# Banded attention in blocks of 32 by 32: a fused attention and MoE kernel on one Trainium2 core

## The chip, the cores and the metric

The kernel runs on one core of a Trainium2 chip. The core has a matrix engine (TensorE, "PE" in the profile, with its weight loads as "PEld"), a vector engine (VectorE, "DVE"), a scalar engine (ScalarE, "ACT"), a general engine (GpSimd, "POOL") and a sync engine (SyncE, "SP") that issues most of the transfers. Matrix products land in eight PSUM banks of 128 partitions by 512 f32 numbers; the other operands lie in SBUF, also 128 partitions. The metric is the device time of one execution in microseconds (us).

## The reference

There are 8 batches of 8 heads, 576 positions and 64 numbers per head. Each head computes two attentions, their sum goes into a feed-forward layer.

```python
# pooled: q, k, v averaged over groups of 4 positions (144 left), full softmax
out_up = np.repeat(sm_attn(q_d, k_d, v_d), 4, axis=2)
# banded: each query sees the keys less than 4 positions away
mask = np.abs(pos[:, None] - pos[None, :]) < 4
scores = np.where(mask, scale * np.matmul(q, k.transpose(0, 1, 3, 2)), -1000000000.0)
scores = scores - np.max(scores, axis=-1, keepdims=True)
attn = np.exp(scores)
attn = attn / (np.sum(attn, axis=-1, keepdims=True) + 1e-09)
x = out_up + np.matmul(attn, v)
# x as 4608 tokens of 512 numbers
h = x @ w_in                                  # 512 -> 2048
return (h * np.clip(h + 3.0, 0.0, 6.0) / 6.0) @ w_out
```

## The kernel before, in words

**Feed-forward layer.** The 4608 tokens go in nine chunks of 512 (`PART`). For each of 16 slices `f` of the 2048 hidden numbers, GEMM1 (`gemm1`, L981) makes a bank `h` from four pieces of the inner dimension, three matmuls each, because every f32 operand is split into a rounded high part and a low part. ACT and DVE apply the gate (L987, L991) and split the result again (L995, L999). GEMM2 (`gemm2`, L1031) adds four token tiles into banks `o0` to `o3`, three matmuls each. That is twelve matmuls of 128x512 per slice for either GEMM, 1728 in all for each. GEMM1 alternates between banks `h0` and `h1`.

**Attention.** A *unit* is one batch and one pair of heads, 32 units in all. The two heads of a unit lie side by side: head 0 in partitions 0 to 63, head 1 in 64 to 127. Batches reach the GEMMs in order: chunk 1 needs batch 1, and so on. `plan_unit` writes out one unit's operations. It knows two ways, set by `ALONE = 2`.

Batches 0 and 1 go *alone*: each step is its own operation. Pooled scores (`scores_d`, L455), banded scores (`scores`: L658 puts the mask into the bank as a matmul, L666 the products), turning the weights by PE (`trans_d` L548, `trans` L691), the two products with v (`pv_d` L633 or L636, `pv` L709), and for some value sums `sum_pe` (L418).

Batches 2 to 7 go by *bursts* (`plan_burst`): one operation on PE holds the scores of a new unit and the products with v of the unit two before it (`DEPTH = 2`), so that GEMMs are interrupted once for both. In it, `scores_d4` (L472) makes pooled scores, `pv` (L709) and `pv_d4` (L617) the products, `scores` (L666) the banded scores. Between a unit's first and second burst the weights are turned: the unnormalised scores become weights on DVE, ACT and POOL, are written to DRAM (`put_d`, `put`) and read back in pieces (`get_d`, `get`), and DVE turns 32x32 blocks (`turn_d` L584, `turn_l` L603). A burst takes `h0` and `h1` for products and a third of the pooled scores, and two more banks `a0` and `a1` for scores. At the change of batch group the pipeline runs full: the first two bursts have no old unit, and the last two no new one.

**The banded windows before.** Ten windows of 64 queries by 64 keys, 57 apart (`window`), cover 576 positions with a margin of three. Five lie in one half of the partitions and five in the other; with two heads that is 20 matmuls of 64 by 64 for the scores and 20 for the products. The softmax of batches 2 to 7 adds the mask while moving out of PSUM (`outside`, L682), takes the maximum over 64 keys (L511), and does one exponential per window with the maximum as bias and the sum as a by-product (`exps_sums`, L522: ten exponentials, ten accumulator reads). `norm` (L539) divides.

**The order of work.** Nothing is ordered by hand. `Plan` holds operations with engines to choose from, costs, resources (banks, SBUF slots) and due times; `emit` plays a schedule forward and writes the instructions in the order it finds. So a change to one cost or resource can reorder everything. `need` and `UNIT_T` set when a batch is due. The planner also models PE's instruction supply (`FETCH`, L1151, `fetch`), in records of matmuls (`rec`).

## Time and profile before

| | |
|---|---|
| median of 3 runs | 926.57 us (925.02 to 932.66) |
| profiled execution | 927.57 us |
| its span | 925.0 us |
| PE busy | 907.6 us (98%), 7045 matmul records |
| DVE busy | 552.5 us (60%) |
| ACT busy | 440.2 us (48%) |
| POOL busy | 233.8 us (25%) |
| DMA moved | 93.48 MB, mean 101 GB/s |
| GEMM2 (L1031), GEMM1 (L981) | 412.7 us, 405.6 us busy |

The span runs from the first instruction to the last; a little of an execution lies around it. Busy time of PE is modelled at the ends of matmuls, so the distance from one start to the next tells more than the busy share. In the chain of waits, followed back from the last instruction, each piece is what the rest waited for, with its start and length. A group such as "L666 x40" is 40 records of line 666.

### The profile page before, as it was taken

To read this page: it belongs to the slowest core of one execution; us is meant where nothing else is said; L and a number is where in the kernel's file an instruction comes from. 1 tells how busy PE (TensorE), PEld (TensorE's weight loads), DVE (VectorE), ACT (ScalarE), POOL (GpSimd) and SP (SyncE) were. 2 spreads that over 40 slices of the span, in tenths; PEclk is the share of its full clock that TensorE was granted. 3 is DMA by queue.
4 is the path that set the end of the run, shared out by engine and by line. 5 is a ranking of instruction groups with operands and counts; after the bars stand their busy time and mean duration, and the time that the engine had idled before them with its cause. 6 is when DMAs were issued, how large, how long until landed. Compare 5 with 4: busy or idle time off the path is not lost.

```text
span 925.0 us, 19239 instructions
## 1 busy us (share of the span) xinstructions
PE 907.6 (98%) x7045; PEld 734.4 (79%) x7045; DVE 552.5 (60%) x979; ACT 440.2 (48%) x1443; POOL 233.8 (25%) x310
## 2 busy tenths in 40 slices
PE   6999999999999999999999999999999999999997
PEld 4567777788878888888888888888888888888886
DVE  6889999666675568456855576556744332233222
ACT  3888747555564456345554445445542222222221
POOL 4553644323352233023402240224201000000000
PEclk9999999999999999999999999999999999999999
DMA  7997533546665455455555456445533010001001
GB/s 205 318 220 255 108 111 74 122 89 134 122 138 113 99 109 123 101 102 108 115 131 104 99 109 139 77 97 110 139 73 57 1 46 1 1 1 46 0 1 45
DMA packets 311757, 93.48 MB, mean 101 GB/s; under 512 B 251376, under 2 KB 297840, under 8 KB 311664
## 3 DMA queue, kind: packets, MB, share of 16 engines
q1 hardware_dynamic: 311280, 91.69, 44.0%
q8 instruction: 55, 0.90, 0.4%
q10 hardware_dynamic: 384, 0.58, 0.2%
q14 instruction: 38, 0.31, 0.1%
HBM read 69.60 MB, written 22.61 MB: 100 GB/s over the span
## 4 chain that ended last, share of the span: by engine, by line
PE 87%; DMA 3%; DVE 3%; ACT 3%; SPq 2%; issue 1%; POOL 1%; ACTq 0%; DVEq 0%; POOLq 0%
PE h L981 40%; PE o L1031 39%; PE a L666 2%; PE h L709 1%; DMA arena<-in_v_dram 1%; PE h L617 1%; ACT arena L522 1%; PE a L472 1%; PE o L636 1%; SPq L340 1%; DMA arena<-in_k_dram 1%; DMA out_dram<-arena 1%; DMA early<-in_v_dram 0%; ACT arena L987 0%; POOL rounded L999 0%
## 5 line engine op out<-in xcount | busy, mean ns | idle before, releaser
L1031 PE MATMUL o<-wp,rounded 128*128 128x512 f32 x1728 | 412.7, 392 | 0.5 <-POOL rounded L999 0.4
L981 PE MATMUL h<-rounded,wp 128*128 128x512 f32 x1728 | 405.6, 390 | 2.8 <-DVE arena L991 1.3
L981 PEld LDWEIGHTS h<-rounded,wp 128*128 128x128 f32 x1728 | 322.9, 188 | 72.0 <-DVE arena L991 1.6
L1031 PEld LDWEIGHTS o<-wp,rounded 128*128 128x128 f32 x1728 | 321.2, 188 | 70.2 <-issue 1.0
L987 ACT ACTIVATE arena<-h 128x512 f32<-128x512 f32 x144 | 85.7, 595 | 195.5 <-PE h L981 183.6
L991 DVE SCALAR_TENSOR_TENSOR arena<-arena,h 128x512 f32<-128x512 f32 x144 | 98.0, 681 | 126.1 <-ACT arena L987 125.8
L999 DVE TENSOR_TENSOR rounded<-arena,rounded 128x512 fp32r<-128x512 f32 x110 | 81.5, 741 | 125.3 <-PE o L1031 105.9
L995 ACT CAST rounded<-arena 128x512 fp32r<-128x512 f32 x144 | 89.0, 618 | 114.6 <-PE o L1031 63.9
L522 ACT ACTIVATE arena<-arena 128x64 f32<-128x64 f32 x240 | 80.3, 337 | 0.2
L999 POOL TENSOR_TENSOR rounded<-arena,rounded 128x512 fp32r<-128x512 f32 x34 | 46.3, 1363 | 77.5 <-ACT rounded L995 40.8
L346 DVE STREAM_TRANSPOSE arena<-arena 128x576 f32<-128x576 f32 x56 | 42.6, 764 | 23.0 <-DMA arena<-in_k_dram 18.2
L539 POOL TENSOR_TENSOR arena<-arena 128x640 f32<-128x640 f32 (+1 forms) x22 | 24.6, 1118 | 123.6 <-DVE arena L532 121.4
L405 POOL TENSOR_TENSOR arena<-arena 32x256 f32<-32x256 f32 (+1 forms) x29 | 22.3, 768 | 114.1 <-DMA arena<-in_v_dram 81.2
L522 ACT ACTIVATION_READ_ACCUMULATOR arena<-arena 128x1 f32 x240 | 45.3, 189 | 0.0
L641 ACT ACTIVATE arena<-h 128x144 f32<-128x144 f32 x24 | 7.0, 291 | 66.9 <-PE h L617 66.9
L406 POOL TENSOR_TENSOR arena<-arena 32x128 f32<-32x128 f32 (+1 forms) x29 | 15.2, 525 | 90.2 <-PE h L617 82.1
L361 POOL TENSOR_TENSOR arena<-arena 128x144 f32<-128x144 f32 x58 | 36.5, 630 | 4.5
L584 DVE STREAM_TRANSPOSE arena<-arena 128x384 f32<-128x384 f32 (+1 forms) x48 | 22.2, 467 | 20.5 <-DMA arena<-pd 20.2
L498 ACT ACTIVATE arena<-arena 128x1 f32<-128x1 f32 (+1 forms) x79 | 15.3, 193 | 38.4 <-DVE arena L511 38.2
L403 DVE TENSOR_REDUCE arena<-arena 128x128 f32<-128x512 f32 (+1 forms) x23 | 24.4, 1060 | 11.7 <-PE h L617 10.9
L603 DVE STREAM_TRANSPOSE arena<-arena 128x640 f32<-128x640 f32 x24 | 20.2, 844 | 16.8 <-DMA arena<-pl 16.7
L666 PE MATMUL a<-arena 64*64 64x64 f32 x1160 | 29.1, 224 | 0.0
(197 smaller groups left out, 816.2 us busy)
## 6 DMA issues: line engine op xcount, KB each, us to landing
rawp<-in_w_in_dram SPq DMA_DIRECT2D x16, 512.0 KB
rawp<-in_w_out_dram SPq DMA_DIRECT2D x16, 512.0 KB
arena<-in_q_dram SPq DMA_DIRECT2D x112, 72.0 KB
arena<-in_k_dram SPq DMA_DIRECT2D x112, 72.0 KB
pl<-arena SPq DMA_DIRECT2D x24, 320.0 KB
arena<-pl SPq DMA_DIRECT2D x96, 80.0 KB
arena<-in_v_dram SPq DMA_DIRECT2D x28, 256.0 KB
out_dram<-arena SPq DMA_DIRECT2D x89, 72.0 KB
```

Of the source, the lines that this page charges most:

```text
L346: nc.vector.transpose(out=qk[kind], in_=qk[kind])
L361: eng.tensor_tensor(t, t, x[:, :, r], op=ALU.add)
L403: eng.tensor_reduce(out=vd, in_=raw.rearrange("p r e -> p e r"), op=ALU.add, axis=AX.X)
L522: nc.scalar.activation(x[:, j], x[:, j], AF.Exp, bias=m[:, j:j + 1], scale=0.125, accum_out=s[:, j:j + 1])
L539: eng.tensor_tensor(x, x, s.unsqueeze(2).broadcast_to(list(x.shape)), op=ALU.mult)
L666: nc.tensor.matmul(st["ps", g][half:half + WIN, jj * D:jj * D + WIN], qk_of("q")[hs, k_first:k_first + WIN], qk_of("k")[hs, k_first:k_firs ...
L981: nc.tensor.matmul(st["ps"], win[f][:, wt, kk * P:(kk + 1) * P], xs[part][:, kk], start=(kk == 0 and i == 0), stop=(kk == NK - 1 and i == ...
L987: nc.scalar.activation(st["t"], st["ps"], AF.Relu, bias=3.0)
L991: nc.vector.scalar_tensor_tensor(out=t, in0=t, scalar=6.0, in1=st["ps"], op0=ALU.min, op1=ALU.mult)
L995: nc.scalar.copy(st["gh"], st["t"])
L999: eng.tensor_tensor(st["gl"], st["t"], st["gh"].bitcast(F32), op=ALU.subtract)
L1031: nc.tensor.matmul(otile[n, m], gt[:, ms], wout[f][:, wt], start=(f == 0 and i == 0), stop=(f == NF - 1 and i == 2),)
```

## The change: banded attention by 24 blocks

From batch 1 on (`ALONE = 1`) units go by bursts, and the banded part is laid out anew.

- **Blocks.** 24 blocks of 32 queries by 32 keys, six in each quarter of 144 positions (`narrow`): `NX = 4` quarters, `NV = 6` blocks each. Quarter `x` lies in partitions 32x to 32x+31. With two heads that is 48 matmuls of 32 by 32 for the scores (`scores_x`) and 48 for the products (`pv_x`), 23 to 28 columns each.
- **Turning.** A 32x32 block turns within its partition quarter, so DVE turns the weights in place (`turn_l` on `st["p"]`), and the way through DRAM (`put`, `get`) goes for the banded weights. The pooled weights still take it. The SBUF ring `PT` goes, `Pl` gets three slots.
- **Banks.** A burst takes four banks: `h0`, `h1`, `a0`, `a1`. Each holds the products of one quarter (`st["px"]`); the banded scores lie in `a0` and `a1` as before, the last third of the pooled scores in one piece per head (`rest`, `pull`). The order in a burst is new pooled scores, old pooled products, new banded scores, old banded products. `add` moves out four quarters in place of two halves.
- **Softmax.** A mask 32 wide (`band(NAR, None)`) is made ahead of the work; the maximum is subtracted (`minus`), then one exponential, one sum on DVE (`exps`, `total`), as batch 0 does, over 384 numbers per partition in place of 640.
- **Planning.** Bursts are booked at `BURST = 2.2, 1.2` in place of 2.4 and 1.35. After batches 1 and 2 the pipeline is emptied (`FLUSH`), and a burst that waits for its `a` banks keeps GEMM1 from taking `h` (`firm`).

The diff, cut to its core:

```diff
@@ -34,6 +34,7 @@
 NAR = 32
+NX, NV, XQ = 4, 6, S // 4
 QS, QSTEP, QB = 64, 40, 48
@@ -51,6 +52,16 @@
     return STEP * j, (0 if j == 0 else HALO), STEP + HALO
+def narrow(x, j):
+    first = (0, XQ - 4, 2 * XQ - 4, S - NAR - (NV - 1) * 23)[x]
+    step = 24 if 0 < x < NX - 1 else 23
+    at = first + j * step
+    lo = x * XQ if j == 0 else at + 4
+    hi = (x + 1) * XQ if j == NV - 1 else at + step + 4
+    return at, lo, hi, first, step
@@ -149,6 +161,7 @@
             nc.vector.tensor_reduce(out=head[:, h:h + 1], in_=ident[:NAR, h * KR:(h + 1) * KR], op=ALU.add, axis=AX.X)
+        band(NAR, None)
@@ -301,24 +314,28 @@
         hx = [(f"h{g}x", key) for g in range(2)]
+        ax = [("a", ("b", key, g)) for g in range(2)]
         def burst():
-            hb = [bank(*h) for h in hx]
+            hb, ab = [bank(*h) for h in hx], [bank(*a) for a in ax]
             if new:
-                new["pooled"](hb)
+                new["pooled"](hb, ab)
             if old:
-                old["pv"](hb)
+                old["pooled"](hb, ab)
             if new:
                 new["banded"]()
+            if old:
+                old["banded"]()
         both = [x for x in (new, old) if x]
-        cost = 2.4 if len(both) == 2 else 1.35
-        o = op("PE", cost, burst, [a for x in both for a in x["after"]], take=hx + [t for x in both for t in x["take"]],
-               free=[t for x in both for t in x["free"]], lag=LAGT, rec=52 * len(both))
+        cost = BURST[0] if len(both) == 2 else BURST[1]
+        o = op("PE", cost, burst, [a for x in both for a in x["after"]], take=hx + ax + [t for x in both for t in x["take"]],
+               free=[t for x in both for t in x["free"]], lag=LAGT, rec=60 * len(both))
+        o.firm = True
         if old:
-            units.pop(0).send((o, hx))
+            units.pop(0).send((o, hx, ax))
         if unit:
-            unit.send((o, hx))
+            unit.send((o, hx, ax))
             units.append(unit)
@@ -370,6 +387,14 @@
+        def ldx(h):
+            if "v" not in st:
+                st["v"] = buf("v", un, [P, NV, ROW])
+            for x in (2 * h, 2 * h + 1):
+                first, step = narrow(x, 0)[3:]
+                nc.sync.dma_start(
+                    st["v"][x * NAR:(x + 1) * NAR], src(v_all, row0 + first, [[ROW, NAR], [step * ROW, NV], [1, ROW]]))
@@ -466,26 +493,24 @@
                 a, n = QPLACE[h][j]
-                for i in range(2 if n == 2 else 1):
-                    ks = slice(i * SD // 2, (i + 1) * SD // 2) if n == 2 else slice(0, SD)
-                    ps = rest(h, i) if n == 2 else rows_d4(n)[a * D:(a + 1) * D]
-                    nc.tensor.matmul(
-                        ps, q4[hs, j * QSTEP:j * QSTEP + QS], k4[hs, ks], start=True, stop=True, skip_group_check=True)
-        def rest(h, i):
-            return st["hb"][h][i * D:(i + 1) * D, HALF + SD:HALF + SD + SD // 2]
+                ps = rest(h) if n == 2 else rows_d4(n)[a * D:(a + 1) * D]
+                nc.tensor.matmul(
+                    ps, q4[hs, j * QSTEP:j * QSTEP + QS], k4[hs], start=True, stop=True, skip_group_check=True)
+        def rest(h):
+            return st["hb"][h][h * D:(h + 1) * D, 2 * XQ:2 * XQ + SD]
...
         def rows_d4(n):
-            return st["pd"][:, 2] if n == 2 else st["ps", n][:, 5 * D:5 * D + SD]
-        def pull(h, i, eng):
+            return st["pd"][:, 2] if n == 2 else st["ps", n][:, NV * NAR:NV * NAR + SD]
+        def pull(h, eng):
...
                 st["pd"] = buf(pk[0], pk[1], [P, 3, SD])
-            copy_on(eng, st["pd"][h * D:(h + 1) * D, 2, i * SD // 2:(i + 1) * SD // 2], rest(h, i))
+            copy_on(eng, st["pd"][h * D:(h + 1) * D, 2], rest(h))
@@ -583,33 +602,19 @@
-        def put():
-            st["dl"] = dram.tile([5 * P, 2 * D], F32, name=f"pl{b}_{hp}", tag=f"pl{b}_{hp}")
-            nc.sync.dma_start(
-                bass.AP(tensor=st["dl"].tensor, offset=st["dl"].offset, ap=[[2 * D, P], [P * 2 * D, 5], [1, 2 * D]]),
-                st["p"].rearrange("p j g k -> p j (g k)"))
-        def get():
-            st["pt"] = buf("PT" + kv, ("l", un), [P, 5, 2 * D])
-            raw = st["pt"].rearrange("p j (h k) -> p (j h) k", k=NAR)
-            for e in range(4):
-                nc.sync.dma_start(
-                    raw[e * NAR:(e + 1) * NAR],
-                    bass.AP(tensor=st["dl"].tensor, offset=st["dl"].offset + e * NAR,
-                            ap=[[2 * D, NAR], [NAR * 2 * D, 20], [1, NAR]]))
         def turn_l():
-            x = st["pt"].rearrange("p j q -> p (j q)")
+            x = st["p"].rearrange("p g j k -> p (g j k)")
             nc.vector.transpose(out=x, in_=x)
-        def pv_d4():
+        def pv_d4(hb, ab):
             st["od"] = buf("od" + k0, un, [P, SD])
-            st["pod"] = [st["px"][g][:, HALF:HALF + SD] for g in range(2)]
+            st["pod"] = [hb[g][:, XQ:XQ + SD] for g in range(2)]
+            st["px"] = [hb[0][:, :XQ], hb[1][:, :XQ]] + [x[:, NV * NAR + SD:NV * NAR + SD + XQ] for x in ab]
             for g in (0, 1, 2):
@@ -646,15 +651,40 @@
         def places():
-            st["p"] = buf(pl[0], pl[1], [P, 5, 2, D])
+            st["p"] = buf(pl[0], pl[1], [P, 5, 2, D] if alone else [P, 2, NV, NAR])
             stats = buf("st" + k0, ("l", un), [P, 2, 12])
-            st["m"], st["s"] = stats[:, 0, :NWIN], stats[:, 1, :NWIN]
+            n = NWIN if alone else 2 * NV
+            st["m"], st["s"] = stats[:, 0, :n], stats[:, 1, :n]
+        def at_of(h, x):
+            return (h + x // 2) % 2
+        def scores_x():
+            for jj in range(NV):
+                for x in range(NX):
+                    first = narrow(x, jj)[0]
+                    for h in range(2):
+                        hs = slice(h * D, (h + 1) * D)
+                        nc.tensor.matmul(
+                            st["ps", at_of(h, x)][x * NAR:(x + 1) * NAR, jj * NAR:(jj + 1) * NAR], qk_of("q")[hs, first:first + NAR],
+                            qk_of("k")[hs, first:first + NAR], start=True, stop=True, skip_group_check=True)
+        def pv_x():
+            for jj in range(NV):
+                for x in range(NX):
+                    first, lo, hi = narrow(x, jj)[:3]
+                    ks = slice(x * NAR, (x + 1) * NAR)
+                    for h in range(2):
+                        nc.tensor.matmul(
+                            st["px"][x][h * D:(h + 1) * D, lo - x * XQ:hi - x * XQ], st["v"][ks, jj, h * D:(h + 1) * D],
+                            st["p"][ks, at_of(h, x), jj, lo - first:hi - first], start=True, stop=True, skip_group_check=True)
-            if alone:
-                places()
-            for g in range(2 if alone else 0):
+            places()
+            for g in range(2):
                 nc.tensor.matmul(
@@ -680,7 +711,7 @@
             nc.vector.tensor_tensor(
-                st["p"][:, :, g], rows(g), mask.unsqueeze(1).broadcast_to([P, 5, D]), op=ALU.add)
+                st["p"][:, g], rows(g), mask[:, :NAR].unsqueeze(1).broadcast_to([P, NV, NAR]), op=ALU.add)
@@ -708,16 +737,16 @@
                             st["px"][g][h * D:(h + 1) * D, at + lo:at + hi], st["v"][ks, jj, h * D:(h + 1) * D],
-                            st["pt"][ks, jj, half + lo:half + hi], start=not direct, stop=True, skip_group_check=True)
-        def add(g):
+                            st["pt"][ks, jj, half + lo:half + hi], start=False, stop=True, skip_group_check=True)
+        def add(x):
...
             nc.vector.tensor_tensor(
-                xt[b][:, hp, g * HALF:(g + 1) * HALF].rearrange("e (q r) -> e q r", r=4),
-                st["px"][g][:, :HALF].rearrange("e (q r) -> e q r", r=4),
-                st["od"].unsqueeze(2)[:, g * SD // 2:(g + 1) * SD // 2].broadcast_to([P, SD // 2, 4]), op=ALU.add)
+                xt[b][:, hp, x * XQ:(x + 1) * XQ].rearrange("e (q r) -> e q r", r=4),
+                st["px"][x].rearrange("e (q r) -> e q r", r=4),
+                st["od"].unsqueeze(2)[:, x * XQ // 4:(x + 1) * XQ // 4].broadcast_to([P, XQ // 4, 4]), op=ALU.add)
@@ -741,16 +765,16 @@
         else:
-            sd, hx = yield {
+            sd, hx, bks = yield {
                 "un": un, "after": turned["q"] + turned["k"] + [pooled["q"], pooled["k"]] + masked,
-                "take": [sk] + bks, "free": [], "pooled": scores_d4, "banded": scores}
+                "take": [sk], "free": [], "pooled": scores_d4, "banded": scores_x}
             sl_op = sd
...
         else:
-            pulls = [op(on("ev", SD // 2), 0, partial(pull, h, i), [sd], take=[pk], free=[hx[h]]) for h in range(2) for i in range(2)]
+            pulls = [op(on("ev", SD), 0, partial(pull, h), [sd], take=[pk], free=[hx[h]]) for h in range(2)]
             sums_d = []
@@ -770,27 +794,22 @@
             for g in range(2):
-                subs.append(op("DVE", 0.49, partial(outside, g), [sl_op] + subs, take=[pl, sl], free=[bks[g]]))
-            a = op("DVE", 0.8, lambda: top(p_all(), st["m"]), subs)
-            a = op("ACT", 0.2, lambda: nc.scalar.activation(st["m"], st["m"], AF.Copy, scale=-0.125), [a])
-            m = a
-            for j in range(0, NWIN, 2):
-                a = op("ACT", 0.62, lambda j=j: exps_sums(j, p_all(), st["m"], st["s"]), [m, a])
-            a = op("ACT", 0.2, lambda: plus(st["s"]), [a])
-        size = 10 * D
-        if alone:
-            a = op("ACT", 0.2 + size / 1150, lambda: exps(p_all(), 0.125), subs)
-            a = op("DVE", 0.15 + size / 960, lambda: total(p_all(), st["s"]), [a])
-            a = op("ACT", 0.2, lambda: plus(st["s"]), [a])
+                subs.append(op("DVE", 0.34, partial(outside, g), [sl_op] + subs, take=[pl, sl], free=[bks[g]]))
+            a = op("DVE", 0.55, lambda: top(p_all(), st["m"]), subs)
+            subs = [op(on("minus", 2 * NV * NAR), 0, lambda eng: minus(eng, p_all(), p_all(), st["m"]), [a], lock=True)]
+        size = 10 * D if alone else 2 * NV * NAR
+        a = op("ACT", 0.2 + size / 1150, lambda: exps(p_all(), 0.125), subs)
+        a = op("DVE", 0.15 + size / 960, lambda: total(p_all(), st["s"]), [a])
+        a = op("ACT", 0.2, lambda: plus(st["s"]), [a])
         a = op("DVE", 0.2, lambda: recip(st["s"]), [a])
...
             back_d = op("SP", 1.0, put_d, [softmax_d], free=[pk], size=dma(3 * P, 576), nd=2)
-            back_l = op("SP", 0.5, put, [softmax], free=[pl], size=dma(5 * P, 512))
+            t = [op("DVE", 0.15 + 2 * NV * NAR / 900, turn_l, [softmax])]
             yield
-        tk_d = ("PT0", ("d", un)) if b == 0 else ("pdt1", un) if alone else ("qk", ("rd", un))
+        tk_d = ("PT0", ("d", un)) if b == 0 else ("qk", ("rd", un))
         ok = ("od" + k0, un)
@@ -818,22 +837,21 @@
             turned_d = [op("DVE", (0.5, 0.3)[i], partial(turn_d, i), [a]) for i in range(2)]
-            a = op("SP", 2.0, get, [back_l], take=[tk], size=dma(20 * P, 128), nd=4)
-            t = [op("DVE", 0.8, turn_l, [a])]
         bks = [(PS, ("x", un, g)) for g in range(2)]
...
         else:
-            a, bks = yield {
+            a, hx, bks = yield {
                 "un": un, "after": t + lv + turned_d + sums, "take": [ok] + xbs,
-                "free": [tk, vk, tk_d, ("vd" + k0, un)], "pv": pv_all}
+                "free": [pl, vk, tk_d, ("vd" + k0, un)], "pooled": pv_d4, "banded": pv_x}
+            bks = hx + bks
             od = op("ACT", 0.29, mean, [a], free=[bks[0]])
...
         else:
-            adds = [op("DVE", 0.45, partial(add, g), [a, od], free=[bks[g]], dl=due) for g in range(2)]
+            adds = [op("DVE", 0.29, partial(add, x), [a, od], free=[bks[x]], dl=due) for x in range(NX)]
             plan.free_after(ok, adds)
@@ -1086,7 +1104,7 @@
     warm = op("DVE", 0.2, make_identb)
-    masked = [warm, op("DVE", 2.3, make_mask)]
+    masked = [warm, op("DVE", 3.0, make_mask)]
     for d in range(2):
@@ -1105,6 +1123,8 @@
             plan_duo(b, d, masked)
+            while d and b in FLUSH and units:
+                plan_burst(None)
             if need_chunk(b) > n:
@@ -1121,11 +1141,13 @@
-ALONE = 2
+ALONE = 1
+BURST = 2.2, 1.2
-DEPTH = 2
+DEPTH, FLUSH = 2, (1, 2)
@@ -1180,7 +1202,7 @@
             ("xb", 2, NHP * S * 4), ("t", 2, TOK * 4), ("ob", 1, 2048), ("raw", 2, 4 * ROW * 4), ("qk", 5, S * 4),
-            ("v", 1, 5 * ROW * 4), ("Pd", 1, 3 * SD * 4), ("Pl", 1, NWIN * D * 4), ("PT", 1, 5 * P * 4), ("vd", 1, 2 * ROW * 4),
+            ("v", 1, NV * ROW * 4), ("Pl", 3, 2 * NV * NAR * 4), ("Pd", 1, 3 * SD * 4), ("vd", 1, 2 * ROW * 4),
             ("od", 1, SD * 4), ("p4", 2, SD * 4), ("st", 4, 2 * 12 * 4)):
```

49 lines of the change are left out of this document (23 added, 26 removed).

## The prediction

> **What bounds the kernel now.** I read the page first, then the busy time by stretches, then the chain of waits, then single bursts in the timeline. The page gives the span and the engines; the stretches (columns: length, then busy time of PE, weight loads, DVE, ACT, POOL with instruction counts, granted clock, DMA share, GB/s) show where PE has room.
>
> ```profile
> span 925.0 us, 19239 instructions
> PE 907.6 (98%) x7045; PEld 734.4 (79%) x7045; DVE 552.5 (60%) x979; ACT 440.2 (48%) x1443; POOL 233.8 (25%) x310
> 65.00:150.00 85.00, 84.64 (x681) 64.37 (x680) 80.69 (x114) 57.95 (x109) 39.66 (x30) 1.00 0.55 144
> 180.00:700.00 520.00, 518.80 (x4425) 428.89 (x4426) 325.35 (x607) 265.97 (x1052) 141.95 (x212) 1.00 0.53 110
> ```
>
> PE is idle 1.2 us of 520 from 180 on, at full granted clock. So what the change is worth there is what it does to PE's own work, and relief of DMA, ACT or DVE alone buys at most that 1.2 us. From 65 to 150, where batch 1 is done, DVE is busy too, 80.69 of 85 us: two engines bound that stretch together.
>
> The profiled run took 927.57 us, 2.57 more than its span, and lies 1.0 above the median of 926.57. I sum against 927.57 and take 1.0 off at the end.
>
> **What batch 1 costs PE today.** The chain of waits through one of its four units (start, length, what):
>
> ```profile
> 103.34 0.32 PE a L418 x2
> 103.66 0.88 PE a L455 x12
> 104.54 2.95 PE h L981 x12
> 107.49 2.72 PE o L1031 x12
> 110.20 0.29 PE a L658 x2
> 110.49 0.74 PE a L666 x40
> 111.24 2.95 PE o L1031 x12
> 114.18 0.66 PE a L548 x6
> 114.84 2.73 PE h L981 x12
> 117.57 0.79 PE a L633 x8
> 118.36 2.98 PE o L1031 x12
> 121.34 0.55 PE a L691 x5
> 121.88 2.75 PE h L981 x12
> 124.64 0.74 PE a L709 x40
> ```
>
> Twelve GEMM matmuls take 2.72, and 2.95 when they follow 64x64 work: the return costs 0.23. The attention rows add to 4.97; the excess of the six GEMM rows over 2.72, with the return after the last row, is about 1.0. So 5.96 per unit, 23.8 for four.
>
> **What a burst costs today.** A full burst (scores of one unit, products of another), then one that holds only products:
>
> ```profile
> 390.56 0.41 PE a L472 x8
> 390.96 0.13 PE h L472 x8
> 391.09 0.58 PE h L709 x40
> 391.67 0.36 PE h L617 x10
> ...
> 392.16 0.58 PE a L666 x29
> 392.74 5.67 PE o L1031 x24
> ```
>
> ```profile
> 704.99 0.74 PE h L709 x40
> 705.72 0.48 PE h L617 x12
> 706.21 2.99 PE o L1031 x12
> ```
>
> Full: 392.74-390.56 = 2.18 plus the 0.23 return, 2.41. Products alone: 1.22+0.23 = 1.45. Scores alone, estimated from the parts 0.54+0.58+0.23: 1.35. Batches 2 to 7 have 24 units, so 22 full bursts and two of each half: 53.0+2.7+2.9 = 58.6. With batch 1: 82.4 us of PE.
>
> **What one set of small matmuls costs.** The timeline of PE (start, span of the group):
>
> ```profile
> 390.49 0.47 PE L472 MATMUL a<-arena 64*64 64x144 f32 x8
> 390.79 0.30 PE L472 MATMUL h<-arena 64*64 64x72 f32 x8
> 390.91 0.76 PE L709 MATMUL h<-arena 64*64 64x60 f32 x40
> 54.00 0.39 PE L418 MATMUL a<-arena,four 64*16 64x128 f32 x2
> 54.31 0.83 PE L455 MATMUL a<-arena 64*64 64x144 f32 x10
> ```
>
> Each f32 matmul leaves two records (20 matmuls, x40). L617's six matmuls of 144 columns (0.48) need two rounds on the four 64x64 tiles, so 0.24 a round. L455 runs six such matmuls on two tiles in three rounds, 0.88 with its entry. So matmuls on different tiles run at once, and a round (one matmul per tile) costs 0.24 at 144 columns and 0.12 at 72 (390.79 to 390.91). L709's 20 matmuls are five rounds of four in 0.58: 0.117 a round with 57 to 60 columns and 64 weights, where columns alone would give 0.097. Something other than columns holds it: the 64 weights, or a floor.
>
> A change of tile shape costs time. L472's 144-column round with the start before it takes 0.30 where 0.24 is work, and GEMM's twelve from 387.68 at 2.72 end at 390.40, 0.09 before 390.49: 0.14 with rounding. From 64x16 to 64x64 tiles the same is seen: L418's two passes of 128 columns are 0.21 by the 144-column price, yet L455 starts 0.31 after them. So I charge 0.14 for each of the two shape changes that the new burst adds (64x64 to 64x32 scores, to 32x64 products).
>
> **The new burst.** Pooled part: 0.54+0.49 as now, plus 0.12, since the third pooled score piece is one matmul of 144 columns per head instead of two of 72. Banded part X = S+V. S: 48 matmuls of 32 weights by 32 columns on eight tiles, six rounds. V: 48 of 64 weights by 23 to 28 columns on eight tiles, six rounds. No row shows eight tiles at once, fewer than 57 columns, or 32 weights, so X is bounded. Lower end: columns alone set the pace, 0.24/144 per column: S = 6x0.053, V = 6x0.040, X = 0.56. Upper end: each record keeps today's 0.58/40 = 14.6 ns, 192 records: X = 2.80. I take weights or columns, whichever is more, as L709's row suggests: S = 6x0.058 = 0.35, V = 6x0.117 = 0.70, X = 1.05.
>
> Full: 0.54+0.12+0.49+0.28+0.23+X = 1.66+X = 2.71. Scores alone 1.03+S; products alone 1.00+V; the pair 2.03+X. The flushes after batches 1 and 2 make three runs of the pipeline: batch 1 has two full and two of each half, the rest 20 full and four of each half.
>
> - Batches 2 to 7: 41.3+24X = 66.5 against 58.6: **+7.9**.
> - Batch 1: 7.4+4X = 11.6 against 23.8: **-12.2** of PE.
>
> With everything kept the break-even is at X = 1.2.
>
> **Whether batch 1's gain is kept.** DVE had 4.3 us of room from 65 to 150. Its rows there and in the bursts:
>
> ```profile
> L539 DVE TENSOR_TENSOR arena<-arena 128x640 f32<-128x640 f32 x4 | 4.3, 1064 | 0.1
> L514 DVE TENSOR_TENSOR arena<-a,arena 128x320 f32<-128x320 f32 x6 | 2.6, 481 | 0.0
> L526 DVE TENSOR_REDUCE arena<-arena 128x10 f32<-128x640 f32 x3 | 2.4, 814 | 1.0 <-ACT arena L517 1.0
> L682 DVE TENSOR_TENSOR arena<-a,mask 128x320 f32<-128x320 f32 x48 | 23.0, 482 | 0.2 <-DMA pl<-arena 0.2
> L584 DVE STREAM_TRANSPOSE arena<-arena 128x384 f32<-128x384 f32 x24 | 13.8, 576 | 4.5 <-DMA arena<-pd 4.3
> ```
>
> Per unit the old path spends two subtractions (0.96), a sum (0.81) and, in that stretch, the norm (1.06) on 640 elements; the new one two masked moves of 192 (0.6 of L682's 0.48, twice: 0.58), a maximum and a sum of 384 (0.49 each) and two more turns (0.58 and about 0.36 for the smaller one). Minus and norm are planned for POOL first. DVE thus comes out near even, a little lighter, while POOL gains some 4 us a unit in a stretch where it is busy 39.66 of 85. Room of 4.3 plus work for batch 2 that can wait covers most of 12 us; I keep 10, with 0 and 12.2 as the ends. The added round trip of the pooled weights per unit of batch 1 lies under chunk 0's GEMMs.
>
> **Costs at nothing.** Leaving out the banded round trip frees queue and DMA, which PE did not wait for. ACT loses ten exponentials and ten accumulator reads per unit:
>
> ```profile
> L522 ACT ACTIVATE arena<-arena 128x64 f32<-128x64 f32 x240 | 80.3, 337 | 0.2
> q8 instruction: 55, 0.90, 0.4%
> ```
>
> That is over 3 us a unit off an engine half busy; I take 1 us of the last idle PE time for it. The second mask adds 0.7 us of DVE by the plan (line 1089) ahead of batch 0, while q, k and v are still being loaded; uncovered it costs those 0.7. Value loads go from three DMAs a unit to four, beside a queue that is no longer asked for the banded round trip. The burst now waits for a0 and a1 as well as h0 and h1, and holds all four until four adds, each about half of today's two, are done. What stands behind it on PE is GEMM2, which needs neither: 24 matmuls, 5.67 in the row at 392.74, run before h is wanted again.
>
> Sum: 927.57+7.9-10-1 = 924.5; less 1.0 for the median, **924**. Own range 918 (all of batch 1 kept, X lower by 0.15) to 934 (none kept).
>
> **Rivals.**
>
> *Columns set the pace* (X = 0.56). For it: the same cells stream 144 and 72 columns in proportion. Against it: 57 columns cost as much as 64 weights would. Batches 2 to 7: 54.7, -3.9; batch 1: 9.6, -14.2, of which I keep 11.5; with ACT's 1: 910 on the median. Chance 0.34.
>
> *A floor per round* (0.117 whatever the size): X = 12x0.117 = 1.40, +16.3, batch 1 -10.8 with 9 kept: 933. The row for it is L709's again. Chance 0.10. [...]
>
> *Weights set it* is my forecast, chance 0.33. [...]
>
> *Four tiles at once, not eight* (ends slower). Place: both banded parts; then 12 rounds each, X = 2.10, +33.1, batch 1 -8: 951. It decides from X = 1.5 on, where 24X-17.3 less some 8.5 from batch 1 and the 1 passes 9.3. For it: no more than four are ever seen at once; against it: two became four without loss. Chance 0.09.
>
> *Instructions come too late* (slower). The 0.90 MB of the q8 row are 55 pieces for twice 7045 records: a piece is 128 matmul records with their loads, and takes 0.4% of 16x925/55 = 1.1 us to move. Today's burst has 108 records and meets one piece's end at most; the new one has 216 and meets two in (216-128)/128 = 69% of the 22 full bursts. Between the two lie 128/216 of 2.71, 1.6 us, enough to move a piece but not for what precedes the move, which no row shows. If the second must wait 1.5 us (between 0 and 2.9, the upper end from the planner's own 4.5 us a piece, line 1151), that is 23 us: 947. For it: those counts; against: no burst here shows a stall. Chance 0.10.
>
> *A pace per instruction*, X = 2.80: +49.9-5.2: 970. Chance 0.04. That the change does not do what it says is not to be seen in the diff.
>
> **Chances.** A measurement of this kernel tells about 1% from no change, 9.3 us: 917 to 936. Faster: 0.31 of the column case and 0.06 of the forecast, 0.37. Slower: 0.09, 0.10 and 0.04, with 0.03 each of the forecast and the floor, 0.29. Same: 0.34. The range goes from 905, below the column case, to 951; outside remain about 0.06 below and 0.12 above.
>
> **What would show it.** In the timeline of the new kernel: a full burst from GEMM to GEMM of 2.5 (2.71 less the return) is my case, 2.0 the column case, 2.8 the floor, 3.5 four tiles; x96 records in each banded part; 0.14 at each change of shape; bursts of one kind with unequal lengths would be the instruction supply. PE idle between 60 and 140 would show that batch 1's gain went to DVE. L522 gone from ACT with no change in PE's idle time would confirm that relief as worthless. The prediction is wrong if PE idles elsewhere by more than 3 us, since then another engine took over.

## The result: 7.7% slower

The changed kernel takes 998.72 us (median of 4 runs, 995.75 to 1001.84), the kernel before, on the same chip, 925.80. The ratio is 1.077, with a 95% interval of 1.070 to 1.084. The prediction was 924, with a range that ended at 951.

The page of the changed kernel's profiled execution (995.75 us, of which 993.9 are the span), in the lines that answer to those of before:

```profile
span 993.9 us, 24822 instructions
PE 945.3 (95%) x10041; PEld 766.4 (77%) x10041; DVE 550.0 (55%) x1078; ACT 365.9 (37%) x927; POOL 265.7 (27%) x351
q8 instruction: 79, 1.29, 0.6%
```

PE went from 7045 to 10041 matmul records, each with a weight load, and the pieces of instructions from 55 to 79. ACT lost 74 us of work. The busy time by stretches:

```profile
65.00:150.00 85.00, 74.06 (x913) 58.13 (x913) 71.15 (x113) 52.21 (x103) 52.88 (x43) 0.94 0.61 142
180.00:700.00 520.00, 500.20 (x6155) 410.88 (x6155) 289.85 (x607) 174.52 (x501) 137.86 (x208) 0.97 0.37 76
```

Two things are new. PE is idle 19.8 us of 520 in the long stretch (1.2 before) and 10.9 of 85 where batch 1 is done (0.4 before). And the granted clock is no longer 1.00 in either.

**A burst without a stall.** The chain of waits through one (start, length, what):

```profile
343.41 0.41 PE a L497 x8
343.81 0.11 PE h L497 x2
...
344.05 0.48 PE h L622 x10
344.53 0.95 PE a L669 x63
345.48 0.18 PE h L680 x4
...
346.43 0.14 PE a L680 x8
346.57 2.94 PE o L1049 x12
```

From the first row to GEMM2 it is 346.57-343.41 = 3.16, where the forecast had 2.48 (2.71 less the return). The pooled part takes 1.12 (forecast 1.15) and the return 2.94-2.72 = 0.22 (0.23). The banded scores take 0.95 and the banded products 1.09, each with its change of tile shape; the forecast had 0.49 and 0.84. With the prediction's 0.14 per change taken off (no run measures that alone), X is 0.81+0.95 = 1.76 in place of 1.05, and the burst 0.68 longer than forecast.

**A burst with a stall.** The same view of another one, and what PE waited for in the whole span (us in total, times, longest):

```profile
387.30 0.14 PE h L680 x5
387.44 0.12 PE a L680 x8
387.56 1.00 issue
388.56 0.23 PE h L680 x2
...
389.14 0.13 PE a L680 x8
389.27 5.94 PE o L1049 x18
```

```profile
PE h L680 <- issue: 13.0, 8, 2.0
PE a L680 <- issue: 8.0, 5, 2.1
PE h L999 <- DVE arena L746: 3.6, 1, 3.6
```

"Issue" is time in which PE waited for nothing that another engine does. Thirteen of the 22 full bursts stop so in their banded products, for 21.0 us together, 1.6 each. In the trace every one of these stops ends 2.30 to 2.68 us after the first packet of a q8 transfer that lies inside the burst.

The places of the stops fit ends of such pieces. Number the instructions that the trace has for PE (matmuls, loads and the few semaphore instructions) from 0 on: the first matmul after each of the 13 stops is number 193 or 194 past a multiple of 256. Fourteen of the 22 full bursts hold two such places, and 13 of them stop at the second; in the one that doesn't, the first lies only 8 instructions into the burst. None of the eight bursts with one such place stops.

**A second cost behind some stalls.** Busy time right after that burst (the seventh number is the granted clock):

```profile
389.00:390.00 1.00, 1.00 (x21) 0.84 (x17) 0.06 (x1) 0.72 (x3) 0.82 (x3) 1.00 0.06 16
390.00:393.40 3.40, 3.40 (x10) 2.65 (x9) 3.39 (x12) 0.00 (x0) 2.43 (x6) 0.50 0.53 106
393.40:394.40 1.00, 1.00 (x6) 0.81 (x5) 0.94 (x2) 0.00 (x0) 0.00 (x0) 0.99 0.35 46
```

For 3.4 us PE runs at half its clock, and eight GEMM matmuls start 427 ns apart in place of 227. The trace has 75 such distances in the changed kernel, 15.0 us, and none after 42 us in the kernel before.

**By stage.** A stage lasts until 384 more GEMM records have started; the last column goes on to the end of the span:

| us | first GEMM | stage 1 | 2 | 3 | 4 | 5 | 6 | 7 | 8 and 9 |
|---|---|---|---|---|---|---|---|---|---|
| before | 42.3 | 122.5 | 101.2 | 97.1 | 96.8 | 96.9 | 96.7 | 92.4 | 179.1 |
| changed | 39.8 | 135.0 | 106.3 | 115.3 | 110.0 | 111.4 | 102.0 | 94.4 | 179.7 |

Stage 1 holds batch 1. The loss of 69 us of span is 12.5 there and most of the rest in stages 3 to 6.

### The profile page after: what moved, and what is told of

The parts are those of the page before. It is cut to its first block, busy times and chain, and to the rows that moved or that the text cites. A ratio compares the mean times of both kernels' runs of the same rounds, so it can differ in the third digit from the quotient of the medians.

```text
span 993.9 us, 24822 instructions
## 1 busy us (share of the span) xinstructions
PE 945.3 (95%) x10041; PEld 766.4 (77%) x10041; DVE 550.0 (55%) x1078; ACT 365.9 (37%) x927; POOL 265.7 (27%) x351
## 2 busy tenths in 40 slices
DMA packets 246883, 81.85 MB, mean 82 GB/s; under 512 B 196849, under 2 KB 232817, under 8 KB 246769
## 3 DMA queue, kind: packets, MB, share of 16 engines
q8 instruction: 79, 1.29, 0.6%
## 4 chain that ended last, share of the span: by engine, by line
PE 88%; issue 4%; DVE 3%; DMA 2%; SPq 2%; POOL 1%; ACT 0%; ACTq 0%; DVEq 0%; POOLq 0%
PE o L1049 39%; PE h L999 38%; PE a L669 2%; PE h L680 2%; PE h L622 2%; PE a L680 1%; PE a L497 1%; DMA arena<-in_v_dram 1%; PE o L641 1%; PE h L497 1%; DMA pd<-arena 0%; DMA early<-in_v_dram 0%; POOL wp L218 0%; DVE arena L363 0%; DVE arena L435 0%
## 5 line engine op out<-in xcount | busy, mean ns | idle before, releaser
L1049 PE MATMUL o<-wp,rounded 128*128 128x512 f32 x1728 | 430.4, 403 | 6.0 <-DVE wp L218 2.9
L1049 PEld LDWEIGHTS o<-wp,rounded 128*128 128x128 f32 x1728 | 332.0, 194 | 80.1 <-DVE wp L218 4.3
L1009 DVE SCALAR_TENSOR_TENSOR arena<-arena,h 128x512 f32<-128x512 f32 x144 | 98.1, 683 | 196.2 <-ACT arena L1005 195.6
L1017 POOL TENSOR_TENSOR rounded<-arena,rounded 128x512 fp32r<-128x512 f32 x40 | 54.9, 1372 | 162.3 <-ACT rounded L1013 89.4
L680 PE MATMUL h<-arena 32*64 32x24 f32 (+3 forms) x1344 | 32.7, 218 | 13.0 <-issue 13.0
L680 PE MATMUL a<-arena 32*64 32x24 f32 (+2 forms) x1344 | 34.0, 219 | 8.0 <-issue 8.0
L680 PEld LDWEIGHTS h<-arena 32*64 32x64 f32 x1344 | 28.7, 130 | 13.7 <-issue 12.8
L649 DVE SCALAR_TENSOR_TENSOR arena<-h,arena 128x144 f32<-128x144 f32 x28 | 8.6, 307 | 53.6 <-ACT arena L131 48.4
L680 PEld LDWEIGHTS a<-arena 32*64 32x64 f32 x1344 | 29.0, 131 | 10.6 <-issue 10.6
L428 DVE TENSOR_REDUCE arena<-arena 128x128 f32<-128x512 f32 (+1 forms) x28 | 29.3, 1046 | 3.3 <-PE h L622 1.8
L218 POOL TENSOR_TENSOR wp<-early,wp 128x1024 fp32r<-128x1024 f32 (+1 forms) x11 | 24.0, 2182 | 25.3 <-ACT wp L214 25.2
```

Source lines behind the costliest of these rows:

```text
L218: eng.tensor_tensor(w[:, :, 1], words["z"], w[:, :, 0].bitcast(F32), op=ALU.subtract)
L428: eng.tensor_reduce(out=vd, in_=raw.rearrange("p r e -> p e r"), op=ALU.add, axis=AX.X)
L680: nc.tensor.matmul(st["px"][x][h * D:(h + 1) * D, lo - x * XQ:hi - x * XQ], st["v"][ks, jj, h * D:(h + 1) * D], st["p"][ks, at_of(h, x), j ...
L1009: nc.vector.scalar_tensor_tensor(out=t, in0=t, scalar=6.0, in1=st["ps"], op0=ALU.min, op1=ALU.mult)
L1017: eng.tensor_tensor(st["gl"], st["t"], st["gh"].bitcast(F32), op=ALU.subtract)
L1049: nc.tensor.matmul(otile[n, m], gt[:, ms], wout[f][:, wt], start=(f == 0 and i == 0), stop=(f == NF - 1 and i == 2),)
```

## The experiments

In what follows, and in the expectations, a burst is measured from 227 ns after the start of the last GEMM matmul ahead of it to the start of the next. That is 0.09 more than the chain's rows: 2.27 in the kernel before and 3.25 in the changed one. The medians of the kernel before lie between 925.7 and 927.4 in every comparison.

### Is it the number of instructions? Half as many of them

Every second block is left out and the others are made twice as wide.

```diff
-            for jj in range(NV):
+            for jj in range(0, NV, 2):
...
-                            st["ps", at_of(h, x)][x * NAR:(x + 1) * NAR, jj * NAR:(jj + 1) * NAR], ...
+                            st["ps", at_of(h, x)][x * NAR:(x + 1) * NAR, jj * NAR:(jj + 2) * NAR], ...
...
```

The products are changed likewise.

> Leaves out every second block of the changed kernel: 24 score matmuls of 32 queries by 64 keys and 24 product matmuls of up to 51 columns per unit, in place of 48 and 48 (the output is then not the reference's). Same tile shapes, same shape changes, same four banks, same batch 1. A full burst then has 120 records, fewer than the 128 of one 16 KB piece of PE's instructions. Instruction supply: no burst can meet the ends of two pieces, so all full bursts are alike, 2.3 to 2.5 us from GEMM to GEMM where they were 3.25 or 4.5 to 5.5; the stalls (21.8 us in the bursts after 150 us) and the half-clock GEMMs behind them (about 13) go too, and the total is about 935. Rival, tile shapes or banks cause the long bursts: they stay uneven by 1.3 to 2.3 us, and the total stays above 965.

Measured: 942.2 us (one run). All 20 full bursts after 170 us take 2.55, with no stop in any of them: from 180 to 800 us the view of waits has no row for PE. After 200 us no GEMM matmul runs at half clock. The chain through one:

```profile
501.37 0.66 PE a L670 x45
502.02 0.20 PE h L683 x4
...
502.71 2.95 PE o L1052 x12
```

The tiles, the changes of shape and the layout are those of the change; the stalls go with the number of instructions. What is left of the loss, 15 us, is stage 1 (133.6) and the 2.55 in place of 2.27.

### The kernel before with as many instructions

The 64x64 scores of a full burst are written again until it has 216 records, and in a second run until it has 160.

```diff
             if new:
                 new["banded"]()
+            if new and old:
+                for _ in range(2):
+                    new["banded"]()
+                new["banded"](14)
```

With 160 records it is `banded()` once and `banded(6)`; the number is how many of the 20 matmuls are written.

> The kernel before, its full bursts lengthened from 108 to 216 records by writing the 64x64 banded scores again (54 more matmuls, the same values). No 32-wide tile anywhere. 54 matmuls at 0.117 per four add 1.58 us to each of 22 bursts, 35 us. Instruction supply: some 60% of the full bursts also stall, for about 1.3 us each since 128 records now take 1.9 us, so 970 to 995 in all, with bursts of 3.85 and of 4.5 to 6. Rival, the 32-wide shapes cause it: every burst 3.85, no stall, 962.

> The kernel before with full bursts of 160 records in place of 108: 26 of the 64x64 score matmuls are written once more. By the theory of pieces of 128 records, a stall comes where two pieces end in one burst, (160-128)/128 = 25% of the 22 full bursts: 5 or 6 stalled (2 to 9), by 0.9 to 2.3 us each; bursts without one take 2.27+52x14.6 ns = 3.03. The whole is 943 without stalls and some 952 with five and the waits behind them. If stalls grew with the length of the burst rather than with the second piece, nearly all 22 would show some.

Measured: 979.5 and 944.6 us (one run each). What PE waited for between 180 and 800 us, with 216 records and then with 160:

```profile
PE a L672 <- issue: 12.9, 12, 2.0
```

```profile
PE a L671 <- issue: 2.6, 3, 1.7
```

Bursts without a stop take 3.89 and 3.07, within 0.04 of what 14.6 ns a record gives. With 216 records 12 of 22 stop, with 160 three, with 120 (the run above) none. So the stalls need no 32-wide matmul. By the rule in the prediction, (n-128)/128 of the bursts, it would be 15, 5.5 and none: the right form, and a little too high. Here too every stop stands at 193 or 194 past a multiple of 256; 15 and 3 bursts hold two such places, and only three of these, whose first place is at most 21 instructions in, do not stop. Here too each stop ends 2.17 to 2.71 us after a q8 transfer starts. Half clock follows only once in the run with 216.

### The same instructions, further apart

First in the changed kernel, then with batch 1 left alone (the run for which the next heading gives the base), old products and new scores become two bursts; the second version, shown here, plans every burst 6 us behind the last. The first one also fills a part of SBUF with zeros at the start.

```diff
+        if unit and len(units) == DEPTH:
+            plan_burst(None)
+        after = last_burst[:]
         new = next(unit) if unit else None
-        old = next(units[0]) if len(units) == DEPTH or units and not unit else None
+        old = next(units[0]) if units and not unit else None
...
-        o = op("PE", cost, burst, [a for x in both for a in x["after"]], ..., lag=LAGT, rec=60 * len(both))
+        o = op("PE", cost, burst, after + [a for x in both for a in x["after"]], ..., lag=6.0 if after else LAGT, rec=60 * len(both))
+        last_burst[:] = [o]
```

> The changed kernel with each full burst cut in two: the old unit's products first, the new unit's scores at least 6 us later, with GEMMs between. 108 records each. Instruction supply: no stall in any burst, 1.68 and 1.82 us as the short bursts of the changed kernel are; an additional entry and return for 22 bursts costs 8 us, the stalls and the half clock save about 38: near 965. Rival, shapes or banks: as many stalls as before, above 1000.

> Batch 1 alone as before, batches 2 to 7 by the new blocks, but the products of the old unit and the scores of the new one as two bursts of 108 records, every burst planned at least 6 us after the one ahead of it. The same 32-wide matmuls are done as in the run with batch 1 alone (980.8 us, 14 of 22 bursts stalled); only their spacing changes. If the stalls come from two pieces of instructions that end too close together: bursts of 1.68 and 1.82, no stall and no half clock after 200 us save where two bursts still fall closer, 24 x (3.50 - 2.27) = 30 us more than the kernel before and some 4 less in the first stage: 945 to 958 us. If the 32-wide matmuls stall or slow TensorE by themselves, whatever the spacing: 975 us or more.

Measured: 992.0 us for the first (one run), far above what was expected. After 200 us no burst stops for instructions; three take 5.0 because GEMM1 stands right behind them and waits 2.9 us for VectorE's adds to free its banks. Besides those waits, stage 1 takes 137.7 us, and 62 GEMM matmuls run at half clock (12.4 us), so it told little of the whole.

The second, 964.9 us (ratio to before 1.042, 1.038 to 1.046), is the clean one. It is 15.9 us faster than the 980.8 of the kernel that does the same matmuls in joint bursts (of which 13 stop, not the 14 of the text above), though two bursts of 1.68 and 1.82 cost 0.25 more than one of 3.25. Its chain through a products burst has no stop:

```profile
359.88 0.64 PE h L628 x12
360.52 0.18 PE h L686 x4
...
361.47 0.14 PE a L686 x8
361.61 4.55 PE o L1063 x19
```

Of the 48 bursts, 44 have exactly 1.68 or 1.82, none shows a wait for "issue", and six GEMM matmuls run at half clock (41 in joint bursts). It missed its range by 7 us, and the GEMMs wait 8.3 us in all where they wait 1.3 with joint bursts; 4.8 of this is GEMM2 waiting for its split operands. The cause of the stalls is thereby shown from three sides, fewer instructions, more of them in the old kernel, and the same ones apart, and by their places in the stream of instructions.

### The changed kernel with batch 1 left alone

```diff
-ALONE = 1
+ALONE = 2
-DEPTH, FLUSH = 2, (1, 2)
+DEPTH, FLUSH = 2, ()
...
+        "PT1": [(xb0 + 1024, 2560)], "P1": [(xb0 + 3584, 2560)], "pdt1": [(xb0 + 6144, 2 * 2 * SD * 4)],
```

Batch 1's weights get places of their own, since the shared ones have become smaller; the steps of its units are those of the kernel before.

> The changed kernel with batch 1 left alone as before and no emptying of the pipeline, so that only batches 2 to 7 go by the new bursts. By the theory that the new bursts cost 0.98 us each without a stall and 1.3 to 2.3 us more where two pieces of instructions end in them: the stage to the 384th GEMM record is again 122 to 124 us (135.0 in the changed kernel), the later ones stay as in the changed kernel (each some 13 to 18 us longer than before), and the whole is 975 to 988 us. If the long tail came from the change in batch 1 (another order of units, the flushes), the later stages would go back towards 97 us and the whole would be below 955 us.

Measured: 980.8 us, ratio 1.062 (1.055 to 1.069). Busy time over its stage 1, in which PE is idle 1.3 us, and what PE waited for from 40 to 900 us:

```profile
40.00:160.00 120.00, 118.70 (x1074) 89.94 (x1065) 107.71 (x163) 85.00 (x169) 52.84 (x45) 1.00 0.60 167
```

```profile
PE a L680 <- issue: 13.4, 7, 2.1
PE h L680 <- issue: 7.6, 6, 1.8
PE h L1007 <- DVE arena L1017: 1.3, 1, 1.3
```

Again 13 bursts stop, for 21.0 us. The ledger of this run closes: against the kernel before, bursts of the measured length cost 23.6: 22x2.71+2x1.38+2x1.70-58.6 = 7.2 by the forecast's prices without the emptying, and 22x0.68+2x0.44+2x0.26 = 16.4 that they are longer than forecast (scores alone 1.68-0.09 = 1.59 where the forecast less the return has 1.15, products alone 1.73 where it has 1.47). Stops cost 21.0 and half clock 41x0.2 = 8.2, and the start and the first stage give back 4.6. That is 48.2 of the 51.5 us between the two spans.

The rest of the change, moving batch 1 to bursts, then costs 17.4 us of span (993.9-976.5), 14.5 of it by the end of stage 1. The forecast had counted on a gain of 10.

### Why batch 1 loses

Three runs took the move apart: the kernel before with only `ALONE = 1`; the same with the pipeline emptied after batches 1 and 2; and the changed kernel without that emptying.

```diff
-ALONE = 2
+ALONE = 1
...
             plan_duo(b, d, masked)
+            while d and b in FLUSH and units:
+                plan_burst(None)
```

> The kernel before with one number changed: batch 1 by the old bursts (64x64 windows, banded weights through DRAM). It isolates the move of batch 1. If PE bounds the stretch to 150 us: four more full bursts of 2.38 in place of 23.8 us, so 14 us faster, 912. If DVE, POOL and the round trips bound it: PE idles there by 5 to 15 us, and the time is 918 to 932, no gain that a few runs can tell.

> The kernel before with only the move of batch 1 from its own steps to bursts, and the pipeline emptied after batches 1 and 2 as in the change; windows of 64x64 as before, bursts of 108 records. The stage up to the 384th GEMM record after the first (42.3 to 164.8 us before, 122.5 us long) is what tells. Theory 1, the loss of batch 1's gain comes from going by bursts as such (the weights' way through DRAM and DVE leave PE waiting): this stage takes 130 to 137 us, PE waits of 1 to 4 us are seen in it, bursts stay at 2.27, and the whole is 932 to 942 us. Theory 2, it comes from the long bursts of 216 records: the stage takes 112 to 118 us and the whole is 915 to 923 us.

> The changed kernel without the emptying of the pipeline after batches 1 and 2; batch 1 still goes by bursts. The first stage (135.0 us to the 384th GEMM record in the changed kernel, 120.2 where batch 1 is left alone) tells. If the move of batch 1 to bursts itself costs there (PE waits for VectorE's adds and turns and for weights): the stage stays at 131 to 138 and the whole is 993 to 1005 us, since four full bursts more come in place of four pairs of halves. If the emptying costs it: the stage falls to 120 to 126 and the whole is 982 to 990 us.

Measured: 963.7 us (ratio 1.039, 1.035 to 1.043), 962.7 (1.040, 1.035 to 1.045) and 1023.8 (1.106, 1.102 to 1.110). All three lie beyond what either theory gave. The first GEMM and stage 1 together end at 194.6, 198.2 and 201.0 us, against 164.8 before and 174.7 in the changed kernel; in the first two the later bursts take 2.27 as ever. So by bursts batch 1 comes too late with the old windows as with the new blocks, whatever the length of the bursts. The emptying, which was suspected, helps the new blocks by 25 us (998.7 against 1023.8) and makes no clear difference with the old windows (962.7 against 963.7). What PE waits for in the second run from 150 to 200 us:

```profile
PE a L472 <- DVE arena L355: 20.4, 2, 15.4
PE h L709 <- DVE arena L532: 8.1, 1, 8.1
PE o L1031 <- ACT wp L201: 6.3, 1, 6.3
```

L355 pools the queries and keys of a new unit. The timeline has SP issue their loads at 175.32 and 177.41, after 32 other DMAs since 158.36, about 0.5 us each: stores and re-loads of the weights, values, outputs. The new blocks take part of those away, and lose less; that the one is the reason for the other wasn't tried. In the changed kernel itself PE is idle 14.2 us of stage 1 (42 to 175):

```profile
42.00:175.00 133.00, 118.82 (x1566) 92.40 (x1565) 113.01 (x191) 85.70 (x189) 79.73 (x73) 0.95 0.67 163
```

VectorE is busy 113 of these 133 us, 85%, and was 93% busy before. So PE does not wait because VectorE is full but because a step that it needs comes late: 3.6 us for an add that frees a bank (L746), 2.9 for the gate of a GEMM1 ahead of a burst (L1009), 3.9 for weights (L218). Which step in the longer way through DRAM makes them late wasn't tried.

### What sets the pace of the small matmuls

Twice the changed kernel with one property of the matmuls altered: the loop over the heads outermost, so that four tiles follow one another in place of eight; and scores with 16 columns in place of 32.

```diff
-            for jj in range(NV):
-                for x in range(NX):
-                    first = narrow(x, jj)[0]
-                    for h in range(2):
+            for h in range(2):
+                for jj in range(NV):
+                    for x in range(NX):
+                        first = narrow(x, jj)[0]
...
```

The loops of the products are turned in the same way.

```diff
-... jj * NAR:(jj + 1) * NAR], ... qk_of("k")[hs, first:first + NAR], ...
+... jj * NAR:jj * NAR + NAR // 2], ... qk_of("k")[hs, first:first + NAR // 2], ...
```

> The changed kernel with the loop over the two heads outermost in the banded scores and products: the same 96 matmuls, but only four tiles follow one another in place of eight. By the theory that 64 weights take 58 ns a load and eight tiles hide one another down to 7.3 ns a record, under a sequencer that gives no record sooner than 8.3 ns: four tiles give 14.6 ns a record for the products, V = 1.40 in place of 0.95, and 7.3 under 8.3, so S stays at 0.80. A full burst without a stall is 3.70 from GEMM to GEMM in place of 3.25, products alone 2.27 in place of 1.82, scores alone 1.68 as it is; the whole is 1003 to 1011 us, less than 28 x 0.45 more since a slower burst gives the instructions more time. If only the count of instructions set the pace: 3.25, 1.82, 1.68 and 999 us.

> The changed kernel with the banded scores cut to the first 16 of each block's 32 keys: the same 96 records with the same 32 weights, each with 16 columns in place of 32 (VectorE reads the half twice, so the second 16 keys of a block get wrong scores). If a pace per instruction sets the scores (8.3 ns a record with its load, whatever its size): the banded scores stay at 0.95 from their first record to the products, a burst with scores alone stays 1.68 from GEMM to GEMM, a full one without a stall 3.25, and the whole 994 to 1003 us. If columns set any of it: up to 0.4 less in each of the 28 bursts with scores, 2.85 and 1.28, and 985 to 990 us.

Measured: 1011.6 us (ratio 1.092, 1.085 to 1.099) and 1001.4 (1.079, 1.070 to 1.088). A full burst without a stall takes 3.56 and 3.23, products alone 2.13 and 1.82, scores alone 1.75 to 1.87 and 1.66 (the 1.75 to 1.87 are above the 1.68 expected, and why isn't known; in full bursts the same scores take no longer). The scores in the chain, four tiles first, then 16 columns:

```profile
604.67 0.95 PE a L669 x74
605.62 0.17 PE h L680 x2
```

```profile
349.29 0.93 PE a L669 x64
350.21 0.18 PE h L680 x4
```

Neither half the tiles nor half the columns moves the scores from 0.95 by more than 0.02. After the first 48 their records start in pairs 16.7 ns apart, 8.3 each, which is 4.2 ns for each matmul and each weight load. The products do follow the tiles: the first 32 start eight in 58.4 ns with eight tiles and four in 58.4 with four, the pace at which the forecast priced 64 weights; after that eight tiles run at 8.3 ns, too. With four they rose by 0.31, less than the 0.45 expected; that the last products of one head and the first of the other overlap is the author's reading, which no row here shows. So after a faster start PE takes one instruction in 4.2 ns, and the 192 of either banded part cost at least 0.8 us. Why the start is faster isn't shown.

### A try for the kernel before

The run with batch 1 alone had a shorter first stage, so its places for batch 1's weights were put into the kernel before.

```diff
...
-        "pdt1": [(xb0 + (2 + i) * S * 4, 2 * 2 * SD * 4) for i in range(2)],
+        "PT1": [(xb0 + 1024, 2560)], "P1": [(xb0 + 3584, 2560)], "pdt1": [(xb0 + 6144, 2 * 2 * SD * 4)],
```

> The kernel before with places of their own in SBUF for the banded weights and the turned weights of batch 1, in place of the single places shared with batch 2; windows, bursts and instructions as before. The run with batch 1 alone and the new blocks had these places, started its first GEMM at 40.1 us in place of 42.3 and took 120.2 us in place of 122.5 for its first stage. If the places are the cause: 921 to 924 us. If the new blocks' lighter work for batch 2 is the cause: 926 us as before.

Measured: ratio 1.0001 (0.9984 to 1.0018). Stage 1 takes 121.9, so the places aren't the cause. No run beat the kernel before.

## Why the prediction was wrong

**The cost of the banded part, "I take weights or columns, whichever is more": too low by 0.71.** X is 1.76, not 1.05, and past the break-even of 1.2 that the prediction names. It lies inside the bounds of 0.56 and 2.80, but the choice between them rested on rows of 64x64 tiles that never ran faster than 14.6 ns a record. That 32 weights take half of what 64 do, 0.058 a round, was the author's estimate and is shown by no run: after their first 48 records the scores start 8.3 ns apart, which is 0.13 a round. On eight tiles the products do load weights at the pace assumed, eight in 58.4 ns, but only 32 times; then the limit is the rate of instructions. The rival "a pace per instruction" named the mechanism and priced it at 14.6 ns a record; measured is 8.3. Two other rivals fall with the same rows: eight tiles do work at once, eight products in 58.4 ns against four on four tiles, and a floor of 0.117 per round would have made the scores on four tiles 12x0.117 = 1.40, where they stayed at 0.95. Over 34 bursts the excess is 22x0.68+6x0.44+6x0.26 = 19.2 us.

**"Instructions come too late", chance 0.10: it happened as written.** The rival gave 69% of 22 bursts, 1.5 us each, 23 us; measured are 13 of 22 (59%), 1.6 each, 21.0. The planner's 4.5 us a piece, from which it took the upper end of one stop, is a number of the code that no run shows; the stops end 2.30 to 2.68 us after a q8 transfer starts. Against it stood only that "no burst here shows a stall". That was no evidence: the bursts of before have 108 records and meet one end of a piece at most, by the rival's own count. It should have been the likeliest case, and it should have been added to X, not weighed against it: the two are no alternatives. The kernel's own planner models this supply, but the change gives it `rec=60` for half a burst, where the trace has 108 records (52 for 54 in the kernel before). So it couldn't plan for the stops; no run gave it 108.

**"Whether batch 1's gain is kept": it became a loss.** The ends were 0 and 12.2, and VectorE's room was what the step looked at. VectorE did get lighter, as it said (71.15 of 85 us in place of 80.69), and PE waited all the same, for single steps of a longer way that come late. The bound below nothing was missing. Measured, the move costs 17.4 us of span.

**Half clock: in no step.** It adds 15.0 us.

The banded part, the stops and the half clock, set against the prediction's own sum of 924.5 for the profiled run: 19.2+21.0+15.0 = 55.2 of the 71.3 that are missing. Some 16 are left. PE is idle 12.3 us longer in stage 1 than before (14.2 against 1.9); one stop of 2.0 in it is counted already, and the forecast had given up 2.2 of batch 1's 12.2, so this explains some 8. Where the other 8 are stays open.

**What held.** The count of bursts (22 full, 6 and 6) and of records (216, 96 in each banded part); the pooled part and the return; that columns do not set the pace; that PE alone bounds the kernel from 180 us on; and that the relief of ACT and DMA is worth nothing there: ACT fell from 440.2 to 365.9 us and the bytes moved from 93.48 to 81.85 MB, and PE had next to no wait for either that could go. The signs that the prediction named were the right ones: "bursts of one kind with unequal lengths would be the instruction supply" is what the chains above show, and "PE idle between 60 and 140" came, though not from a full VectorE. PE also idles elsewhere by more than 3 us (19.8 from 180 to 700), the sign that another engine took over; but those waits are "issue", and none did.

## What to carry to other kernels

Count instructions per burst of work, not only array time: in these runs a burst that held the ends of two pieces of 256 instructions stopped at the second in 28 of 32 cases (the changed kernel and the padded ones), and a burst with one end never did. The pieces in the profile's instruction queue tell how long one is (here 79 for 2x10041 matmuls and loads). Splitting a matmul into more and smaller ones paid here only until the rate of instructions was the limit, 4.2 ns each. And costs that rest on different resources are added, not put up as rivals.

## What the runs showed of the hardware

- **Instructions come in pieces of 256, and a stop at the end of one lasts until 2.2 to 2.7 us after a q8 transfer starts.** 1.29 MB in 79 pieces are 16.3 KB each, 2x10041 matmuls and loads over 79 are 254, and all stops stand at one place of a grid of 256 (193 or 194 past a multiple). In the changed kernel 13 of 14 full bursts with two ends of a piece stop at the second, none of eight with one end does. Every stop there and in the padded kernels ends 2.17 to 2.71 us after a q8 transfer starts.
- **Small matmuls with their loads run at 4.2 ns an instruction and no faster for long.** After a faster start of 48 records the scores do so with 16 or 32 columns and on four tiles or eight; the products do on eight, after 32 records.
- **The clock can halve after a short stop.** All changes of clock in the changed kernel's trace lie on one grid of 3.41 us, to about 1 ns. From 60 to 900 us each slow stretch at clock 0.50 follows a piece of this grid in which PE was idle 1.00 to 2.05 us; four pieces with 1.05 to 1.76 us have none behind them. Eight matmuls of 427 ns fill one piece, 3.42 us. There are 75 slow matmuls in the changed kernel and 7 in the padded one with 216 records, whose 12 stops are shorter, 1.1 us on the mean in place of 1.6: there only one piece of the grid, idle for 1.98 us, has a slow one behind it, and those up to 1.40 have none. The stop that ends at 308.77 lies across a border, 0.66 and 0.68 us on its two sides, and has no slow stretch behind it either. What decides between 1.0 and 1.8 us is open.
